# Forming the leaky-ReLU activation in place in PSUM for every tile, with both float32r parts read from there

## The chip, the cores and the metric

One Trainium2 chip; the program runs on one of its cores. The metric is the device time of one execution in microseconds (us). The engines are TensorE (PE, with its weight loads PEld), VectorE (DVE), ScalarE (ACT), GpSimd (POOL) and SyncE (SP), which issues all the DMAs. Each of them works through its own queue in order; semaphores tie the queues together.

## What is computed

A two-step packed attention for 8 batches of 8 heads (576 tokens, head dimension 64, 32 packing queries), and behind it a feed-forward layer with a leaky ReLU whose slope alpha differs by feature:

```python
def _attn_ref(q, k, v, p):
    p_packed = sm_attn(p, k, v)                 # softmax attention of the 32 packing queries
    return sm_attn(q, p_packed, p_packed)       # then of the 576 queries over the 32 results

def _moe_ref(x, w_in, w_out, alpha):            # x: 4608 x 512, w_in: 512 x 2048, w_out: 2048 x 512
    h = x @ w_in
    g = np.maximum(h, 0.0) + alpha * np.minimum(h, 0.0)
    return g @ w_out
```

## The kernel before

The feed-forward layer is cut into 256 tiles (k, f): k is one of 16 half batches of 288 tokens (HS), f one of 16 blocks of 128 features. `first` computes a tile's h into a PSUM tile `ps_h`, of which there are two (`ps_h` pool, bufs=2), forms the activation from it, and splits it into two float32r parts, gh (high) and gl (low, the remainder). `second` multiplies both parts by the split output weights and adds into the four PSUM tiles acc0 to acc3: for each of four column blocks two matmuls with gh (L516, L517) and one with gl (L518), 12 a tile. `first` takes 6 matmuls a tile (L480 to L482), each of 288 columns; in the 32 tiles of batch 0 (k < 2) it takes two float32 matmuls (L468) in their place.

The activation of a tile is formed in one of two ways, by the tile's place i in the order:

- i < 32: DVE computes neg = min(h, 0) * alpha (L487) and g = max(h, 0) + neg (L491), both from ps_h, g into SBUF.
- otherwise: ACT computes neg = Relu(-h) (L495) and g = Relu(h) (L496), both from ps_h into SBUF, and DVE g = neg * (-alpha) + g (L497), all in SBUF.

Then ACT casts g to gh (L502), and gl = g - gh (L504) is POOL's for i < 48 and DVE's from there on. ps_h is free for the tile after next when its last reader is done: the second DVE step in the first way, the second Relu in the other.

Beside the tiles run generators that the main loop steps by the table `plan`: `w_out_steps` and `packed_w(..., True)`, which turn the 64-bit weights into two float32r parts (`convert`: ACT L117, L119, L133, DVE L120, L123, L127, L131, L134) during the first 32 tiles; `attention` for the batches ahead, with its splits on POOL (xl L173, vs L275, a_l L392), its softmax steps on DVE, ACT and POOL (L371, L378), and its score sums on DVE (s and s_t, L211); and `packed_w`, which multiplies the attention's results into the input weights (pw), which `split_pw` splits into pwh (DVE L456) and pwl (L458, POOL for k < 4, else DVE).

The loop emits first(i) and then second(i - 2) (AHEAD = 2). The order in which an engine gets its instructions is not the order of the code: the tile framework's scheduler places each instruction by its own timeline of when operands and buffers come free.

Of the kernel before, what the change touches and what calls it, by code (L numbers as in the profile page):

```python
# [8 lines left out]
F32 = mybir.dt.float32  # L9
# [3 lines left out]
AF = mybir.ActivationFunctionType  # L13
ALU = mybir.AluOpType
# [8 lines left out]
def fv(ap):  # L23

    return ap.bitcast(F32)
# [3 lines left out]
def pack_attention_ffn_kernel(  # L29
# [20 lines left out]
    nc = tc.nc  # L50

    B, NP, P, S = qT.shape
    N = pT.shape[-1]
    KT = (S + P - 1) // P
    HS = S // 2
# [18 lines left out]
    gp = ctx.enter_context(tc.tile_pool(name="gp", bufs=2))  # L74
    op = ctx.enter_context(tc.tile_pool(name="op", bufs=2))
# [13 lines left out]
    al = const.tile([P, NF], F32, name="al")  # L89
    nal = const.tile([P, NF], F32, name="nal")  # L90
# [360 lines left out]
    def split_pw(k, h):  # L451

        src = pw[k // 2, h // 2][:, :, (h % 2) * 256 : (h % 2) * 256 + 256]
        th = pwj.tile([P, 2, 256], F32R, name="pwh", tag="pwh")
        tl = pwj.tile([P, 2, 256], F32R, name="pwl", tag="pwl")
        nc.vector.tensor_copy(out=th, in_=src)  # L456
        eng = nc.gpsimd if k < 4 else nc.vector
        eng.tensor_tensor(out=tl, in0=src, in1=fv(th), op=ALU.subtract)  # L458
        pj[k, h] = (th, tl)

    def first(k, f):
        tok = slice((k % 2) * HS, (k % 2) * HS + HS)
        ps = ps_h.tile([P, 512], F32, name="ps_h", tag="h")
        if k < 2 * XF:
            th, a_f = pw[k // 2, f // 4], result[k // 2]
            fs = slice((f % 4) * P, (f % 4) * P + P)
            for i in range(2):
                nc.tensor.matmul(  # L468
                    ps[:, :HS], th[:, i, fs], a_f[:, i, tok], start=(i == 0), stop=(i == 1)
                )  # L470
        else:
            a_h, a_l = result[k // 2]
            key = (0 if k < 2 else k, f // 2)
            if key not in pj:
                split_pw(*key)
            th, tl = pj[key]
            fs = slice((f % 2) * P, (f % 2) * P + P)
            for i in range(2):
                hi, lo = (i == 0), (i == 1)
                nc.tensor.matmul(ps[:, :HS], th[:, i, fs], a_h[:, i, tok], start=hi, stop=False)  # L480
                nc.tensor.matmul(ps[:, :HS], th[:, i, fs], a_l[:, i, tok], start=False, stop=False)  # L481
                nc.tensor.matmul(ps[:, :HS], tl[:, i, fs], a_h[:, i, tok], start=False, stop=lo)  # L482
        i = order.index((k, f))
        neg = gp.tile([P, HS], F32, name="neg", tag="neg")
        g = gp.tile([P, HS], F32, name="g", tag="g")
        if 0 <= i < 32:
            nc.vector.tensor_scalar(  # L487
                out=neg, in0=ps[:, :HS], scalar1=0.0, scalar2=al[:, f : f + 1],
                op0=ALU.min, op1=ALU.mult,
            )  # L490
            nc.vector.scalar_tensor_tensor(  # L491
                out=g, in0=ps[:, :HS], scalar=0.0, in1=neg, op0=ALU.max, op1=ALU.add
            )
        else:
            nc.scalar.activation(out=neg, in_=ps[:, :HS], func=AF.Relu, scale=-1.0)  # L495
            nc.scalar.activation(out=g, in_=ps[:, :HS], func=AF.Relu)  # L496
            nc.vector.scalar_tensor_tensor(  # L497
                out=g, in0=neg, scalar=nal[:, f : f + 1], in1=g, op0=ALU.mult, op1=ALU.add
            )
        gh = gp.tile([P, HS], F32R, name="gh", tag="gh", bufs=3)  # L500
        gl = gp.tile([P, HS], F32R, name="gl", tag="gl", bufs=3)
        nc.scalar.copy(out=gh, in_=g)  # L502
        eng = nc.gpsimd if 0 <= i < 48 else nc.vector
        eng.tensor_tensor(out=gl, in0=g, in1=fv(gh), op=ALU.subtract)  # L504
        gs[k, f] = (gh, gl)

    def second(k, f):
# [32 lines left out]
    order = [(h, 4 * j + f) for j in range(NJ) for h in range(2) for f in range(4)]  # L540
# [27 lines left out]
            yield  # L568

    nc.sync.dma_start(out=al, in_=alpha)  # L570
    nc.vector.tensor_scalar(out=nal, in0=al, scalar1=-1.0, scalar2=None, op0=ALU.mult)

    w0 = packed_w([0], units(*range(NJ)), True)
    drain(zipped(attention(0, 0, True), after(3, attention(0, 1, True))))
# [22 lines left out]
    order = [(h, 4 * j + f) for j in range(NJ) for h in range(2) for f in range(4)]  # L597
    order += [(k, f) for k in range(2, 2 * B) for f in range(NF)]
    AHEAD = 2
    for i in range(len(order) + AHEAD):  # L600
        now = [gen for t, gen, n in plan for _ in range(max(1, -n)) if t <= i and (n < 0 or (i - t) % n == 0)]
        for gen in now[0::2]:
            next(gen, None)
        if i < len(order):
            first(*order[i])
        for gen in now[1::2]:
            next(gen, None)
        if i >= AHEAD:
            second(*order[i - AHEAD])
# [35 lines left out]
```

## Time and profile before

| | us |
|---|---|
| median of 3 runs | 842.3 (841.11 to 844.02) |
| the profiled execution | 844.03 |
| its span, first to last instruction | 842.0 |
| PE busy (matmuls) | 788.6 (94%) |
| DVE busy | 661.8 (79%) |
| ACT busy | 545.1 (65%) |
| POOL busy | 260.1 (31%) |

The shares are means over stages with different limits: in the 40 equal slices of the span DVE is at nine tenths or more from 21 us to 168 us and again in single slices between 270 and 590 us, POOL in the one slice from 232 to 253 us, and PE in nearly all slices from 210 us to the end (not around 390 and 580 us). The chain of work that ended last runs 69% of the span over PE and 16% over DVE. The granted TensorE clock is at nine tenths or more in all slices but the second and the third; over the span it is 0.978. The times in the rows further down are all of this one execution.

### The profile page before, as it was taken

To read this page: it belongs to the slowest core of one execution; us is meant where nothing else is said; L and a number is where in the kernel's file an instruction comes from. 1 tells how busy PE (TensorE), PEld (TensorE's weight loads), DVE (VectorE), ACT (ScalarE), POOL (GpSimd) and SP (SyncE) were. 2 spreads that over 40 slices of the span, in tenths; PEclk is the share of its full clock that TensorE was granted. 3 is DMA by queue.
4 is the path that set the end of the run, shared out by engine and by line. 5 is a ranking of instruction groups with operands and counts; after the bars stand their busy time and mean duration, and the time that the engine had idled before them with its cause. 6 is when DMAs were issued, how large, how long until landed. Compare 5 with 4: busy or idle time off the path is not lost.

```text
span 842.0 us, 15167 instructions
## 1 busy us (share of the span) xinstructions
PE 788.6 (94%) x5384; PEld 733.9 (87%) x5384; DVE 661.8 (79%) x1287; ACT 545.1 (65%) x1333; POOL 260.1 (31%) x251
## 2 busy tenths in 40 slices
PE   5489989898999999998999999997999999999997
PEld 3257767787799999998999999997999999999997
DVE  4999999965788857889989848889889656666663
ACT  5767656556776796667676787665665874545443
POOL 2122234667895511344335302244232100000000
PEclk9879999999999999999999999999999999999999
DMA  9766755556623582312122572211000640000000
GB/s 305 271 213 223 242 184 192 184 157 211 205 68 111 156 244 75 89 46 69 42 61 71 179 238 83 71 57 52 34 16 29 206 148 1 30 1 29 1 30 28
DMA packets 55386, 97.97 MB, mean 116 GB/s; under 512 B 5136, under 2 KB 32784, under 8 KB 55312
## 3 DMA queue, kind: packets, MB, share of 16 engines
q1 hardware_dynamic: 55312, 97.02, 36.0%
q8 instruction: 42, 0.69, 0.4%
q14 instruction: 32, 0.26, 0.1%
HBM read 79.18 MB, written 17.83 MB: 115 GB/s over the span
## 4 chain that ended last, share of the span: by engine, by line
PE 69%; DVE 16%; ACT 6%; DMA 4%; issue 3%; POOL 1%; SPq 1%; ACTq 0%; DVEq 0%; POOLq 0%
PE acc L516 13%; PE acc L518 13%; PE acc L517 13%; PE ps_h L482 6%; PE ps_h L480 6%; PE ps_h L481 6%; DVE g L497 2%; PE ps_h L468 2%; PE ps_m L435 2%; DVE gl L504 1%; PE ps_m L437 1%; PE ps_m L316 1%; PE ps_m L436 1%; DVE mag L127 1%; DVE pwl L458 1%
## 5 line engine op out<-in xcount | busy, mean ns | idle before, releaser
L516 PE MATMUL acc<-gh,wo 128*128 128x288 f32 x1024 | 301.0, 303 | 6.6 <-ACT gh L502 3.9
L517 PE MATMUL acc<-gh,wo 128*128 128x288 f32 x1024 | 296.3, 297 | 0.0
L518 PE MATMUL acc<-gl,wo 128*128 128x288 f32 x1024 | 263.2, 299 | 2.4 <-DVE gl L504 1.7
L516 PEld LDWEIGHTS acc<-gh,wo 128*128 128x128 f32 x1024 | 193.1, 189 | 15.3 <-ACT gh L502 6.2
L517 PEld LDWEIGHTS acc<-gh,wo 128*128 128x128 f32 x1024 | 193.3, 189 | 2.4
L502 ACT CAST gh<-g 128x288 fp32r<-128x288 f32 x256 | 110.1, 433 | 124.0 <-DVE g L497 107.3
L518 PEld LDWEIGHTS acc<-gl,wo 128*128 128x128 f32 x1024 | 179.4, 189 | 7.8 <-DVE gl L504 3.3
L504 DVE TENSOR_TENSOR gl<-g,gh 128x288 fp32r<-128x288 f32 x208 | 123.9, 598 | 60.3 <-ACT gh L502 56.8
L497 DVE SCALAR_TENSOR_TENSOR g<-neg,nal,g 128x288 f32<-128x288 f32 x224 | 133.5, 598 | 38.1 <-ACT g L496 36.9
L480 PE MATMUL ps_h<-a_h,pwh 128*128 128x288 f32 x448 | 132.9, 297 | 0.4 <-DVE pwh L456 0.4
L481 PE MATMUL ps_h<-a_l,pwh 128*128 128x288 f32 x448 | 132.4, 296 | 0.0
L482 PE MATMUL ps_h<-a_h,pwl 128*128 128x288 f32 x448 | 131.7, 295 | 0.0
L495 ACT ACTIVATE neg<-ps_h 128x288 f32<-128x288 f32 x224 | 92.2, 412 | 50.5 <-PE ps_h L482 46.8
L173 POOL TENSOR_TENSOR xl<-xraw,xh 128x576 fp32r<-128x576 f32 x48 | 72.5, 1512 | 153.9 <-ACT xh L172 151.9
L496 ACT ACTIVATE g<-ps_h 128x288 f32<-128x288 f32 x224 | 91.1, 408 | 14.5 <-DVE gl L504 12.9
L480 PEld LDWEIGHTS ps_h<-a_h,pwh 128*128 128x128 f32 x448 | 84.7, 189 | 1.5 <-DVE pwh L456 0.7
L481 PEld LDWEIGHTS ps_h<-a_l,pwh 128*128 128x128 f32 x448 | 84.7, 189 | 0.3
L482 PEld LDWEIGHTS ps_h<-a_h,pwl 128*128 128x128 f32 x448 | 84.3, 189 | 0.4
L458 DVE TENSOR_TENSOR pwl<-pw,pwh 128x512 fp32r<-128x512 f32 x96 | 76.1, 793 | 5.4
L456 DVE CAST pwh<-pw 128x512 fp32r<-128x512 f32 x112 | 61.5, 552 | 12.2 <-PE ps_h L481 9.4
L443 ACT COPY pw<-ps_m 64x512 f32<-64x512 f32 x112 | 65.0, 581 | 7.0 <-PE ps_m L437 5.6
L504 POOL TENSOR_TENSOR gl<-g,gh 128x288 fp32r<-128x288 f32 x48 | 45.0, 947 | 68.1 <-ACT gh L502 65.0
(116 smaller groups left out, 1154.0 us busy)
## 6 DMA issues: line engine op xcount, KB each, us to landing
w<-w_split SPq DMA_DIRECT2D x64, 512.0 KB, 4.1
xraw<-in_kT SPq DMA_DIRECT2D x32, 288.0 KB, 2.9
xraw<-in_qT SPq DMA_DIRECT2D x32, 288.0 KB, 2.9
outT<-ot SPq DMA_DIRECT2D x64, 144.0 KB, 1.8
vraw<-in_v SPq DMA_DIRECT2D x32, 256.0 KB, 2.9
wraw<-in_w_out SPq DMA_DIRECT2D x16, 512.0 KB, 4.1
wraw<-in_w_in SPq DMA_DIRECT2D x16, 512.0 KB, 5.0
w_split<-w SPq DMA_DIRECT2D x16, 512.0 KB, 3.8
```

The source lines that it names most:

```text
L458: eng.tensor_tensor(out=tl, in0=src, in1=fv(th), op=ALU.subtract)
L480: nc.tensor.matmul(ps[:, :HS], th[:, i, fs], a_h[:, i, tok], start=hi, stop=False)
L481: nc.tensor.matmul(ps[:, :HS], th[:, i, fs], a_l[:, i, tok], start=False, stop=False)
L482: nc.tensor.matmul(ps[:, :HS], tl[:, i, fs], a_h[:, i, tok], start=False, stop=lo)
L495: nc.scalar.activation(out=neg, in_=ps[:, :HS], func=AF.Relu, scale=-1.0)
L496: nc.scalar.activation(out=g, in_=ps[:, :HS], func=AF.Relu)
L497: nc.vector.scalar_tensor_tensor(out=g, in0=neg, scalar=nal[:, f : f + 1], in1=g, op0=ALU.mult, op1=ALU.add)
L502: nc.scalar.copy(out=gh, in_=g)
L504: eng.tensor_tensor(out=gl, in0=g, in1=fv(gh), op=ALU.subtract)
L516: nc.tensor.matmul(acc[o][:, :HS], wo_t[f][:, 0, os_], gh, start=begin, stop=False)
L517: nc.tensor.matmul(acc[o][:, :HS], wo_t[f][:, 1, os_], gh, start=False, stop=False)
L518: nc.tensor.matmul(acc[o][:, :HS], wo_t[f][:, 0, os_], gl, start=False, stop=end)
```

## The change

In all 256 tiles the activation is now formed in one way: ACT computes neg = Relu(-h) from ps_h into SBUF (L486), DVE computes neg * (1 - alpha) + h with ps_h as its second operand and writes the result back to ps_h (L487), ACT casts gh from ps_h (L492), and DVE computes gl from ps_h and gh (L493). The second Relu, the SBUF tile g, the way with two DVE steps and POOL's gl are gone. The constant nal becomes 1 - alpha in the one instruction that made -alpha. ps_h is free for the tile after next when gl is done.

```diff
-        i = order.index((k, f))
         neg = gp.tile([P, HS], F32, name="neg", tag="neg")
-        g = gp.tile([P, HS], F32, name="g", tag="g")
-        if 0 <= i < 32:
-            nc.vector.tensor_scalar(
-                out=neg, in0=ps[:, :HS], scalar1=0.0, scalar2=al[:, f : f + 1],
-                op0=ALU.min, op1=ALU.mult,
-            )
-            nc.vector.scalar_tensor_tensor(
-                out=g, in0=ps[:, :HS], scalar=0.0, in1=neg, op0=ALU.max, op1=ALU.add
-            )
-        else:
-            nc.scalar.activation(out=neg, in_=ps[:, :HS], func=AF.Relu, scale=-1.0)
-            nc.scalar.activation(out=g, in_=ps[:, :HS], func=AF.Relu)
-            nc.vector.scalar_tensor_tensor(
-                out=g, in0=neg, scalar=nal[:, f : f + 1], in1=g, op0=ALU.mult, op1=ALU.add
-            )
+        g = ps[:, :HS]
+        nc.scalar.activation(out=neg, in_=g, func=AF.Relu, scale=-1.0)
+        nc.vector.scalar_tensor_tensor(
+            out=g, in0=neg, scalar=nal[:, f : f + 1], in1=g, op0=ALU.mult, op1=ALU.add
+        )
         gh = gp.tile([P, HS], F32R, name="gh", tag="gh", bufs=3)
         gl = gp.tile([P, HS], F32R, name="gl", tag="gl", bufs=3)
         nc.scalar.copy(out=gh, in_=g)
-        eng = nc.gpsimd if 0 <= i < 48 else nc.vector
-        eng.tensor_tensor(out=gl, in0=g, in1=fv(gh), op=ALU.subtract)
+        nc.vector.tensor_tensor(out=gl, in0=g, in1=fv(gh), op=ALU.subtract)
...
-    nc.vector.tensor_scalar(out=nal, in0=al, scalar1=-1.0, scalar2=None, op0=ALU.mult)
+    nc.vector.tensor_scalar(out=nal, in0=al, scalar1=-1.0, scalar2=1.0, op0=ALU.mult, op1=ALU.add)
```

The scheduler makes another order of this. In the rows that follow, square brackets name the engines (or DMA queues) whose semaphores an instruction waits for. PE's queue before, in the last half batch (k = 15): ps_h_11060 is the h of f = 14, wo12 the output weights of f = 12.

```order
L518 MATMUL acc3_10719<-gl_10985,wo11_1214 128x288
L480 MATMUL ps_h_11060<-a_h_7829,pwh_11061 128x288 [waits Activation_49]
L481 MATMUL ps_h_11060<-a_l_7830,pwh_11061 128x288
L482 MATMUL ps_h_11060<-a_h_7829,pwl_11062 128x288
L480 MATMUL ps_h_11060<-a_h_7829,pwh_11061 128x288
L481 MATMUL ps_h_11060<-a_l_7830,pwh_11061 128x288
L482 MATMUL ps_h_11060<-a_h_7829,pwl_11062 128x288
L516 MATMUL acc0_10716<-gh_11016,wo12_1312 128x288 [waits Activation_49]
L517 MATMUL acc0_10716<-gh_11016,wo12_1312 128x288
L516 MATMUL acc1_10717<-gh_11016,wo12_1312 128x288
L518 MATMUL acc0_10716<-gl_11017,wo12_1312 128x288 [waits DVE_49]
```

The same place now: ps_h_10614 is the h of f = 15, wo13 the output weights of f = 13.

```order
L505 MATMUL acc3_10265<-gh_10568,wo13_1397 128x288
L506 MATMUL acc3_10265<-gh_10568,wo13_1397 128x288
L480 MATMUL ps_h_10614<-a_h_7551,pwh_10585 128x288 [waits DVE_49]
L481 MATMUL ps_h_10614<-a_l_7552,pwh_10585 128x288
L482 MATMUL ps_h_10614<-a_h_7551,pwl_10586 128x288
L480 MATMUL ps_h_10614<-a_h_7551,pwh_10585 128x288
L481 MATMUL ps_h_10614<-a_l_7552,pwh_10585 128x288
L482 MATMUL ps_h_10614<-a_h_7551,pwl_10586 128x288
L507 MATMUL acc0_10262<-gl_10569,wo13_1397 128x288
L507 MATMUL acc1_10263<-gl_10569,wo13_1397 128x288
L507 MATMUL acc2_10264<-gl_10569,wo13_1397 128x288
L507 MATMUL acc3_10265<-gl_10569,wo13_1397 128x288
```

Before, first waits for ACT (the second Relu of the tile that had the bank) and stands ahead of the whole second step of the tile two back. Now it waits for DVE (gl of that tile) and stands between that tile's gh matmuls and its gl matmuls; in most of the 256 tiles the order reads gh x8, first x6, gl x4.

DVE's queue among the first 32 tiles before, where the weights are converted beside them (mag is the convert's working tile, w and wo its low parts, pt the attention's result):

```order
L491 SCALAR_TENSOR_TENSOR g_1025<-ps_h_1021,neg_1024 128x288 [waits DVE_49,Pool_49]
L127 SCALAR_TENSOR_TENSOR mag_841<-wraw13_839,mag_841 128x512 [waits DMAHW0_49,DVE_49]
L123 TENSOR_SCALAR mag_873<-mag_873 128x512 [waits DVE_49]
L120 TENSOR_SCALAR mag_946<-mag_946 128x512 [waits Activation_49]
L131 ISA mag_841<-mag_841,low_843 128x1024 [waits DVE_49]
L127 SCALAR_TENSOR_TENSOR mag_873<-wraw14_871,mag_873 128x512 [waits DMAHW2_49,DVE_49]
L123 TENSOR_SCALAR mag_946<-mag_946 128x512 [waits DVE_49]
L487 TENSOR_SCALAR neg_1082<-ps_h_1079,al_108 128x288 [waits PE_49]
L131 ISA mag_873<-mag_873,low_875 128x1024 [waits DVE_49]
L134 TENSOR_TENSOR w_849<-mag_841,w_849 128x512 [waits DMAHW7_49,Activation_49]
L127 SCALAR_TENSOR_TENSOR mag_946<-wraw11_944,mag_946 128x512 [waits DMAHW3_49,DVE_49]
L491 SCALAR_TENSOR_TENSOR g_1083<-ps_h_1079,neg_1082 128x288 [waits DVE_49,Pool_49]
```

and now:

```order
L493 TENSOR_TENSOR gl_859<-ps_h_852,gh_858 128x288 [waits PE_49,Activation_49]
L487 SCALAR_TENSOR_TENSOR ps_h_896<-neg_899,nal_109,ps_h_896 128x288 [waits Activation_49]
L131 ISA mag_833<-mag_833,low_835 128x1024 [waits DVE_49]
L120 TENSOR_SCALAR mag_864<-mag_864 128x512 [waits Activation_49]
L123 TENSOR_SCALAR mag_864<-mag_864 128x512 [waits DVE_49]
L120 TENSOR_SCALAR mag_936<-mag_936 128x512 [waits Activation_49]
L127 SCALAR_TENSOR_TENSOR mag_864<-wraw14_862,mag_864 128x512 [waits DMAHW1_49,DVE_49]
L123 TENSOR_SCALAR mag_936<-mag_936 128x512 [waits DVE_49]
L355 TENSOR_TENSOR pt_112<-p2f_114,pt_112 128x64 [waits Activation_49] x2
L493 TENSOR_TENSOR gl_903<-ps_h_896,gh_902 128x288 [waits PE_49,Activation_49]
L131 ISA mag_864<-mag_864,low_866 128x1024 [waits DVE_49]
L127 SCALAR_TENSOR_TENSOR mag_936<-wraw11_934,mag_936 128x512 [waits DMAHW6_49,DVE_49]
```

Of the two DVE steps of a tile the first waited for PE and the other for DVE and POOL; now the first waits for ACT's neg, the second, gl, for ACT's gh, and convert steps stand between them as before.

POOL's queue from the first tile on, before (t, a_l and vs are the attention's tiles, vraw a raw v):

```order
L504 TENSOR_TENSOR gl<-g,gh 128x288 x9
L181 MEMSET vraw 64x128
L504 TENSOR_TENSOR gl<-g,gh 128x288 x2
L181 MEMSET vraw 64x128
L504 TENSOR_TENSOR gl<-g,gh 128x288 x5
L371 TENSOR_TENSOR t_1074<-t_1074,m_1076 128x576
L504 TENSOR_TENSOR gl<-g,gh 128x288 x2
L378 TENSOR_TENSOR t_1074<-t_1074,z_1128 128x576
```

and now:

```order
L181 MEMSET vraw 64x128 x2
L371 TENSOR_TENSOR t_1062<-t_1062,m_1064 128x576
L378 TENSOR_TENSOR t_1062<-t_1062,z_1115 128x576
L181 MEMSET vraw 64x128
L392 TENSOR_TENSOR a_l<-s_948,a_h 128x576
L181 MEMSET vraw 64x128
L275 TENSOR_TENSOR vs<-vraw,vs 128x5x128
```

The 48 gl are gone from POOL; what is left are the attention's steps and the zeroing of vraw's ends.

## Rows read from the trace of the kernel before

**Rows 1.** Windows: busy us (instructions) of PE PEld DVE ACT POOL, clock, DMA, GB/s.

```profile
44.00:173.00 129.00, 117.20 (x610) 90.44 (x610) 125.19 (x244) 82.10 (x176) 49.44 (x48) 0.93 0.64 208
173.00:250.00 77.00, 69.98 (x472) 62.27 (x471) 54.95 (x103) 52.92 (x132) 62.88 (x59) 1.00 0.53 166
250.00:372.00 122.00, 121.01 (x880) 118.57 (x880) 96.34 (x184) 90.26 (x223) 42.95 (x40) 1.00 0.40 121
372.00:402.00 30.00, 27.28 (x201) 26.35 (x200) 28.68 (x50) 20.05 (x52) 15.42 (x13) 1.00 0.23 70
402.00:566.00 164.00, 162.63 (x1188) 158.93 (x1188) 134.96 (x265) 114.56 (x293) 49.21 (x46) 1.00 0.33 101
566.00:592.00 26.00, 21.35 (x137) 20.35 (x136) 25.03 (x40) 14.91 (x38) 13.27 (x9) 0.90 0.20 58
592.00:665.00 73.00, 73.00 (x537) 72.08 (x536) 62.26 (x126) 48.12 (x125) 18.77 (x17) 0.99 0.16 53
665.00:842.00 177.00, 171.19 (x1267) 169.54 (x1266) 101.94 (x213) 94.13 (x238) 0.00 (x0) 0.99 0.12 41
```

**Rows 2.** Lines by shape, whole span: busy us, mean ns, idle before.

```profile
L497 DVE SCALAR_TENSOR_TENSOR g<-neg,nal,g 128x288 f32<-128x288 f32 x224 | 133.5, 598 | 38.1 <-ACT g L496 36.9
...
L504 DVE TENSOR_TENSOR gl<-g,gh 128x288 fp32r<-128x288 f32 x208 | 123.9, 598 | 60.3 <-ACT gh L502 56.8 <-PE ps_h L482 0.9 <-PE acc L518 0.9
...
L487 DVE TENSOR_SCALAR neg<-ps_h,al 128x288 f32<-128x288 f32 x32 | 16.0, 502 | 0.9 <-PE ps_h L468 0.8
...
L491 DVE SCALAR_TENSOR_TENSOR g<-ps_h,neg 128x288 f32<-128x288 f32 x32 | 14.2, 445 | 0.3
```

**Rows 3.** Lines by shape, DVE, 665 to 842 us.

```profile
L497 DVE SCALAR_TENSOR_TENSOR g<-neg,nal,g 128x288 f32<-128x288 f32 x69 | 35.5, 514 | 22.0 <-ACT g L496 21.8
L504 DVE TENSOR_TENSOR gl<-g,gh 128x288 fp32r<-128x288 f32 x70 | 32.9, 472 | 32.3 <-ACT gh L502 30.8 <-PE ps_h L482 0.9
```

**Rows 4.** Lines by shape, DVE, 566 to 592 us.

```profile
L504 DVE TENSOR_TENSOR gl<-g,gh 128x288 fp32r<-128x288 f32 x7 | 5.0, 718 | 0.7 <-ACT gh L502 0.5
L497 DVE SCALAR_TENSOR_TENSOR g<-neg,nal,g 128x288 f32<-128x288 f32 x7 | 4.6, 662 | 0.0
...
L211 DVE TENSOR_TENSOR s_t<-ps_m,lo 64x288 f32<-64x288 f32 x4 | 1.7, 446 | 0.1
```

**Rows 5.** Lines by shape, DVE, 372 to 402 us.

```profile
L497 DVE SCALAR_TENSOR_TENSOR g<-neg,nal,g 128x288 f32<-128x288 f32 x10 | 7.0, 708 | 0.0
L504 DVE TENSOR_TENSOR gl<-g,gh 128x288 fp32r<-128x288 f32 x8 | 6.0, 754 | 0.4 <-ACT gh L502 0.4
```

**Rows 6.** Lines by shape, 173 to 250 us, DVE, then POOL.

```profile
L497 DVE SCALAR_TENSOR_TENSOR g<-neg,nal,g 128x288 f32<-128x288 f32 x17 | 16.1, 963 | 1.5 <-ACT g L496 1.4
...
L504 POOL TENSOR_TENSOR gl<-g,gh 128x288 fp32r<-128x288 f32 x18 | 15.4, 875 | 3.8 <-ACT gh L502 3.8
```

**Rows 7.** Lines by shape, DVE, 0 to 44 us, then 44 to 173.

```profile
L127 DVE SCALAR_TENSOR_TENSOR mag<-wraw,mag 128x512 uint32<-128x512 uint32 x6 | 4.0, 674 | 0.0
L123 DVE TENSOR_SCALAR mag<-mag 128x512 uint32<-128x512 uint32 x8 | 3.9, 500 | 0.1
...
L127 DVE SCALAR_TENSOR_TENSOR mag<-wraw,mag 128x512 uint32<-128x512 uint32 x26 | 20.1, 775 | 0.0
...
L123 DVE TENSOR_SCALAR mag<-mag 128x512 uint32<-128x512 uint32 x24 | 15.3, 636 | 0.0
```

**Rows 8.** Lines by shape, POOL, 44 to 173 us.

```profile
L504 POOL TENSOR_TENSOR gl<-g,gh 128x288 fp32r<-128x288 f32 x30 | 29.6, 990 | 64.3 <-ACT gh L502 61.2 <-PE acc L517 2.9
```

**Rows 9.** Timeline, DVE, ACT: start, duration (us), instruction, idle before.

```profile
573.51 1.65 DVE L497 SCALAR_TENSOR_TENSOR g<-neg,nal,g 128x288 f32<-128x288 f32 x1
...
575.19 0.43 ACT L502 CAST gh<-g 128x288 fp32r<-128x288 f32 x1 [2.66 <-DVE g L497]
```

**Rows 10.** Timeline, ACT, a tile in the last stage.

```profile
700.41 0.41 ACT L495 ACTIVATE neg<-ps_h 128x288 f32<-128x288 f32 x1 [0.18 <-PE ps_h L482]
...
701.71 0.43 ACT L502 CAST gh<-g 128x288 fp32r<-128x288 f32 x1 [0.59 <-DVE g L497]
```

## The prediction, made before the changed kernel ran

> **What bounds the kernel now.** I read the table of windows first, since no share over the whole span says what one stage is worth [rows 1]. From 665 us on PE is the bound: 1267 matmuls in 171.2 us of 177, 135 ns each, and the rest is the last output's way out. 250 to 372, 402 to 566 and 592 to 665 us look the same: PE is idle for 1.0, 1.4 and 0.0 us. Four stretches are different. From 44 to 173 us DVE is busy for 125.2 of 129 us and PE idle for 11.8: DVE sets the pace of the first 32 tiles, as it converts the weights beside them. From 173 to 250 us POOL is busy for 62.9 of 77 us and PE idle for 7.0. From 372 to 402 and from 566 to 592 us DVE is busy for 28.7 of 30 and 25.0 of 26 us, and PE idle for 2.7 and 4.7. That is 28.6 us of idle PE in all between 44 and 665 us; the matmuls' recorded spans overlap, so short gaps between them are hidden and the true loss is somewhat larger. No change to the activation can win much more than that, and after 665 us it can win nothing.
>
> Then I read what the activation's steps cost, by line and shape [rows 2], and the same lines stage by stage. Both DVE steps with two SBUF operands, g (L497) and gl (L504), average 598 ns; where POOL is silent they take 514 and 472 [rows 3], from 566 to 592 us 662 and 718 [rows 4], from 372 to 402 us 708 and 754 [rows 5], from 173 to 250 us g takes 963 [rows 6]. So POOL stretches them. The steps that read one operand from PSUM are not stretched: s_t at 64x288, in the same 26 us in which gl takes 718, takes 446 [rows 4], and over the run g from ps_h (L491) takes 445 and neg from ps_h, with a pointer scalar, 502 [rows 2].
>
> **The change part by part.**
>
> New g. One SBUF tensor (neg), one PSUM tensor, a pointer scalar, and its output goes to PSUM. No row shows a DVE write to PSUM. Bounds: 445 ns (L491, PSUM in, no pointer) and 963 (the dearest g, rows 6); nothing suggests less than 445, since the length is the same 288. I take 502, the nearest row: PSUM in, a pointer scalar, the same length.
>
> New gl: one PSUM tensor, one SBUF tensor, out to SBUF. L491 is that form: 445 ns, so I take 445; the upper bound is the old quiet 472.
>
> The Trainium skill speaks against this. Its page "VectorE: DVE Perf Modes", section "The TRN2 errata — SBUF-src ops pay a fixed extra latency per instruction", prices a PSUM-source DVE instruction 62 cycles of 0.96 GHz above an SBUF-source one, an estimated 65 ns. By it the 17 g and 15 gl of the two crowded stretches would save 2 us less, and the sum would come out at about 828. The rows show 445 with one operand in PSUM against 472 with both in SBUF, so I do not take it.
>
> First 32 tiles, 44 to 173 us. DVE loses neg (502) and g (445) and gets g (502) and gl (445): nothing, net. ACT gets one neg a tile, 32 x 0.41 = 13 us on 82 of 129 busy: covered, if its queue is not late. What POOL does there stretches the convert's DVE steps. Two of their five lines, here and before 44 us [rows 7]: L127 775 against 674, x26, L123 636 against 500, x24: 2.6 + 3.3 = 5.9 us of stretch. POOL loses 30 gl of 990 ns, 29.6 of its 49.4 us [rows 8], 60% of its work, so about 3.5 us of these come back, and perhaps as much again on the three lines not counted. Against it stands that DVE, in order, now waits for ACT's gh between g and gl: in the quiet stretch 30.8 us over 70 tiles, 0.44 each [rows 3]; here converts stand between the two in the queue and cover it. I take 6 of the 11.8 us.
>
> Tiles 32 to 47, 173 to 250 us. POOL loses 18 gl, 15.4 of its 62.9 us [rows 1, 6]. DVE gets 18 x 0.445 = 8.0 and loses 17 x (963 - 502) = 7.8 on g: even. ACT loses a 0.41 us step a tile. POOL is no longer the bound, DVE at 55 of 77 is not either. I take 6 of PE's 7.0 us and of the short gaps that the records hide.
>
> Tiles from 48 on. In the two crowded stretches DVE saves 10 x (708 - 502) + 8 x (754 - 445) = 4.5 us [rows 5] and 7 x (662 - 502) + 7 x (718 - 445) = 3.0 us [rows 4], 7.5 us where PE is idle for 7.4. A place in point: at 573.5 us one g takes 1.65 us and ACT stands 2.66 us waiting for it [rows 9]. I take 6. Elsewhere in this stage DVE and ACT (one step fewer, 0.41 us a tile) get slack that PE does not need: 0. After 665 us: 0.
>
> nal gets a second operation in its one instruction: 0. The pool g gives up its SBUF: 0.
>
> Sum: 6 + 6 + 6 = 18 us off the profiled execution's 844.0 gives **826.0 us**. That execution lies 1.7 us above the median of the runs, 842.3; the sum is not finer than that.
>
> **Rivals.**
>
> *The bank is held too long (slower).* Before, the second Relu frees the ps_h bank; now gl does, three hand-overs later. There are two banks. PE's order, shown above with the change, turns round: first waited for ACT and stood ahead of the second step of the tile two back; now it waits for DVE's gl and stands behind that tile's gh matmuls. From the end of first to its own gh matmuls there were 36 matmuls, now 22: 4.9 us and 3.0 us at 135 ns. To the reuse of the bank there are 30, 4.0 us, and that now has to hold neg, g, gh and gl: 0.41 + 0.50 + 0.43 + 0.45 = 1.8 us in the quiet stretch, with the bounds taken above for g and gl [rows 2, 3, 10], so the tail is safe. In the crowded stages a tile takes about 2.9 us, so the bank gives 2 x 2.9 less first's 6 x 0.135, 5.0 us. It decides from the point where the chain exceeds 5.0 us; each us beyond costs 0.5 us a tile. A chain that twice meets a wait like the 2.66 us above takes 7.1 us and costs 1.05 us. If one in seven of the some 140 tiles between 250 and 665 us does, that is 21 us; with 12 won earlier and nothing in the crowded stretches the time is 844 - 12 + 21 = 853. For it: two banks, and queues that are in order on both sides. Against it: g and gl themselves no longer stretch, ACT has a third less to do for a tile. The same case covers a dear write to PSUM: at 963 ns the 32 first tiles alone lose 15 us. The Trainium skill's page "PSUM — Partial Sum Buffer", summary of rules, says to evacuate promptly, which is this rival in one word.
>
> *The first stage gives nothing (small gain).* DVE's order there is bound to ACT twice a tile in place of once. With 0.3 us of uncovered wait on each of 32 tiles the 6 us turn to a loss of 3, and some of the rest goes too: 844 + 3 - 10 = 837.
>
> *All idle PE comes back.* 844.0 - 28.6 = 815, and the hidden gaps carry it to about 808.
>
> *It does nothing that can be measured.* The gains above and the bank's waits cancel: 842.
>
> **How the numbers follow.** The forecast (818 to 834) gets 0.43, the small gain (834 to 839.8) 0.20, all idle PE (below 818) 0.12, no difference 0.08, the bank 0.17. A measurement of this kernel can tell about 0.3% from no change, 839.8 to 844.8 around the median. Faster is 0.43 + 0.20 + 0.12 = 0.75, the same 0.08, slower 0.17. The range has to leave out no more than 0.2: from 810 (half of the third case out, 0.06) to 848 (two thirds of the bank's case out, 0.11).
>
> **What would show it.** g and gl near 500 and 445 ns in every stage, with and without POOL beside them; the convert's L123 and L127 nearer to 500 and 674; POOL below 50 of 77 us from 173 to 250 us; the stage up to the 32nd tile about 6 us shorter; no change in the pace of the last 64 tiles. Wrong if g into PSUM is above 600 ns, or if waits of first (L480) on DVE's gl show up as idle PE between 250 and 665 us.

## The result, and the profile after

The changed kernel takes 832.7 us (median of 4 runs, 831.57 to 834.60) beside 843.2 us for the kernel before on the same chip: a ratio of 0.9877, 95% interval 0.9844 to 0.9910, so 10.5 us less. The profiled execution is 834.6 us with a span of 832.8 (before 844.0 and 842.0).

The windows of the kernel after, with the edges of [rows 1] and their columns (us, then busy us of PE, PEld, DVE, ACT, POOL with instructions, clock, DMA share, GB/s):

```profile
44.00:173.00 129.00, 120.60 (x633) 92.97 (x632) 117.36 (x251) 94.28 (x215) 25.83 (x22) 0.95 0.66 217
173.00:250.00 77.00, 73.36 (x513) 67.66 (x512) 55.40 (x128) 49.39 (x120) 44.95 (x43) 1.00 0.50 161
250.00:372.00 122.00, 120.01 (x869) 116.88 (x868) 88.67 (x187) 79.65 (x184) 46.58 (x43) 1.00 0.39 121
...
402.00:566.00 164.00, 158.95 (x1146) 154.69 (x1145) 125.37 (x275) 103.66 (x245) 58.01 (x53) 0.99 0.33 104
566.00:592.00 26.00, 26.00 (x202) 26.00 (x201) 19.69 (x45) 13.96 (x37) 7.06 (x8) 1.00 0.10 33
...
665.00:833.00 168.00, 161.75 (x1211) 160.48 (x1210) 100.81 (x207) 57.20 (x144) 0.00 (x0) 1.00 0.05 19
```

Beside [rows 1]: PE does 633 and 513 instructions in the first two stretches, where it did 610 and 472. From 250 to 372 and from 402 to 566 us it does fewer than before, 869 for 880 and 1146 for 1188, although DVE and ACT have less to do there. The gap at 566 to 592 us is gone, and others have opened.

The costliest groups of the page after (line, engine, operation, tiles and shape, count | busy us, mean ns | idle time before them and what ended it):

```profile
L505 PE MATMUL acc<-gh,wo 128*128 128x288 f32 x1024 | 289.6, 302 | 11.0 <-ACT gh L492 7.9
...
L505 PEld LDWEIGHTS acc<-gh,wo 128*128 128x128 f32 x1024 | 193.0, 189 | 24.1 <-ACT gh L492 15.8
...
L493 DVE TENSOR_TENSOR gl<-ps_h,gh 128x288 fp32r<-128x288 f32 x256 | 115.4, 452 | 72.1 <-ACT gh L492 70.4
L487 DVE SCALAR_TENSOR_TENSOR ps_h<-neg,nal,ps_h 128x288 f32<-128x288 f32 x256 | 132.0, 516 | 44.9 <-ACT neg L486 43.3
```

g took 598 ns and takes 516, gl 598 and 452 [rows 2]. PE waits longer for ACT's gh at the first matmuls of `second`: 15.8 us before the weight loads of L505, where the same place of the kernel before (L516) had 6.2:

```profile
L516 PEld LDWEIGHTS acc<-gh,wo 128*128 128x128 f32 x1024 | 193.1, 189 | 15.3 <-ACT gh L502 6.2
```

Where in the run the time went is read from the ends of the 256 casts to gh (one a tile, in order; tile 0 is the first). The table holds the end of that cast for tiles 31, 48 and 255, and the two differences; all kernels of the study but the pair with a third bank stand in it, since it is read again below. Each row is one execution, the profiled one; 28 executions of the kernel before, taken beside e7, e9 and e11, spread from 839.9 to 848.1 us, so a difference of two or three us in one row says little.

| kernel | way in tiles 0-31 / 32-47 / 48-255 | tile 31 | tile 48 | tile 255 | 31 to 48 | 48 to 255 |
|---|---|---|---|---|---|---|
| before | old, POOL gl / old, POOL gl / old | 178.9 | 250.4 | 833.4 | 71.4 | 583.0 |
| after | in place in all | 178.2 | 242.0 | 824.9 | 63.8 | 583.0 |
| e1 | g to SBUF in all | 179.0 | 247.8 | 822.5 | 68.8 | 574.7 |
| e2 | old, gl always on DVE | 182.0 | 251.5 | 843.8 | 69.6 | 592.3 |
| e3 | in place / in place / old | 175.7 | 240.8 | 824.2 | 65.0 | 583.5 |
| e4 | old / old / in place | 178.3 | 247.3 | 830.6 | 69.0 | 583.3 |
| e6 | g to SBUF / in place / in place | 177.6 | 246.4 | 828.9 | 68.8 | 582.5 |
| e7 | two DVE steps, DVE gl / in place / in place | 184.5 | 253.2 | 837.6 | 68.7 | 584.4 |
| e8 | in place / in place / g to SBUF | 176.9 | 240.7 | 812.5 | 63.8 | 571.8 |
| e9 | old / in place / in place | 180.5 | 251.2 | 832.8 | 70.7 | 581.6 |
| e11 | as e8, but gl reads ps_h | 175.7 | 239.5 | 829.6 | 63.8 | 590.1 |

Before against after: tile 31 ends 0.7 us earlier, tile 48 8.4 us, tile 255 8.5 us. Nearly all of the gain shows between tiles 31 and 48, and 208 of the 256 tiles win nothing.

### The profile page after: what moved, and what is told of

It is laid out like the page before. It is cut to its first block, busy times and chain, and to the rows that moved or that the text cites. A ratio compares the mean times of both kernels' runs of the same rounds, so it can differ in the third digit from the quotient of the medians.

```text
span 832.8 us, 14967 instructions
## 1 busy us (share of the span) xinstructions
PE 786.3 (94%) x5384; PEld 731.3 (88%) x5384; DVE 610.6 (73%) x1303; ACT 486.6 (58%) x1141; POOL 208.7 (25%) x203
## 4 chain that ended last, share of the span: by engine, by line
PE 71%; DVE 14%; DMA 6%; ACT 5%; issue 2%; SPq 1%; POOL 0%; ACTq 0%; DVEq 0%
PE acc L505 14%; PE acc L506 13%; PE acc L507 13%; PE ps_h L480 6%; PE ps_h L482 6%; PE ps_h L481 6%; PE ps_h L468 2%; PE ps_m L435 2%; PE ps_m L437 2%; PE ps_m L436 2%; DVE ps_h L487 2%; DMA wraw<-in_w_in 1%; PE ps_m L316 1%; DVE pwl L458 1%; DVE mag L127 1%
## 5 line engine op out<-in xcount | busy, mean ns | idle before, releaser
L505 PE MATMUL acc<-gh,wo 128*128 128x288 f32 x1024 | 289.6, 302 | 11.0 <-ACT gh L492 7.9
L506 PE MATMUL acc<-gh,wo 128*128 128x288 f32 x1024 | 283.4, 295 | 0.0
L505 PEld LDWEIGHTS acc<-gh,wo 128*128 128x128 f32 x1024 | 193.0, 189 | 24.1 <-ACT gh L492 15.8
L507 PE MATMUL acc<-gl,wo 128*128 128x288 f32 x1024 | 205.9, 301 | 0.0
L492 ACT CAST gh<-ps_h 128x288 fp32r<-128x288 f32 x256 | 102.5, 401 | 123.8 <-DVE ps_h L487 113.2
L486 ACT ACTIVATE neg<-ps_h 128x288 f32<-128x288 f32 x256 | 105.6, 413 | 109.0 <-PE ps_h L482 103.0
L493 DVE TENSOR_TENSOR gl<-ps_h,gh 128x288 fp32r<-128x288 f32 x256 | 115.4, 452 | 72.1 <-ACT gh L492 70.4
L487 DVE SCALAR_TENSOR_TENSOR ps_h<-neg,nal,ps_h 128x288 f32<-128x288 f32 x256 | 132.0, 516 | 44.9 <-ACT neg L486 43.3
L507 PEld LDWEIGHTS acc<-gl,wo 128*128 128x128 f32 x1024 | 159.3, 188 | 3.5
L480 PE MATMUL ps_h<-a_h,pwh 128*128 128x288 f32 x448 | 133.5, 298 | 0.3 <-DVE gl L493 0.2
L480 PEld LDWEIGHTS ps_h<-a_h,pwh 128*128 128x128 f32 x448 | 84.1, 188 | 2.0 <-DVE gl L493 1.0
L456 DVE CAST pwh<-pw 128x512 fp32r<-128x512 f32 x112 | 54.9, 493 | 29.9 <-PE ps_h L481 27.7
L275 POOL TENSOR_TENSOR vs<-vraw,vs 128x640 fp32r<-128x640 f32 x24 | 38.6, 1610 | 42.3 <-ACT vs L274 41.7
L435 PE MATMUL ps_m<-w,pt 128*128 128x512 f32 (+1 forms) x80 | 33.8, 422 | 12.9 <-ACT w L133 10.6
```

The source lines that it names most:

```text
L486: nc.scalar.activation(out=neg, in_=g, func=AF.Relu, scale=-1.0)
L487: nc.vector.scalar_tensor_tensor(out=g, in0=neg, scalar=nal[:, f : f + 1], in1=g, op0=ALU.mult, op1=ALU.add)
L493: nc.vector.tensor_tensor(out=gl, in0=g, in1=fv(gh), op=ALU.subtract)
L505: nc.tensor.matmul(acc[o][:, :HS], wo_t[f][:, 0, os_], gh, start=begin, stop=False)
L506: nc.tensor.matmul(acc[o][:, :HS], wo_t[f][:, 1, os_], gh, start=False, stop=False)
L507: nc.tensor.matmul(acc[o][:, :HS], wo_t[f][:, 0, os_], gl, start=False, stop=end)
```

## The experiments

Two theories went in, A and B in the expectations. A, *DVE and POOL work:* the gain is POOL's gl gone and DVE's steps out of POOL's way. B, *held bank:* on top of that, holding ps_h until gl gives part of it back. Ratios are to the kernel before on the same chip.

**e1: g to SBUF in all tiles**, so that the bank is free after g.

```diff
-        g = ps[:, :HS]
-        nc.scalar.activation(out=neg, in_=g, func=AF.Relu, scale=-1.0)
+        g = gp.tile([P, HS], F32, name="g", tag="g")
+        nc.scalar.activation(out=neg, in_=ps[:, :HS], func=AF.Relu, scale=-1.0)
         nc.vector.scalar_tensor_tensor(
-            out=g, in0=neg, scalar=nal[:, f : f + 1], in1=g, ...
+            out=g, in0=neg, scalar=nal[:, f : f + 1], in1=ps[:, :HS], ...
```

> The changed kernel, but DVE writes g to an SBUF tile in place of ps_h; gh and gl are made from there. The bank is free after DVE's g, two hand-overs earlier than in the changed kernel, and gl has two SBUF operands again. Theory A (the win comes from DVE's and POOL's work alone, the bank costs nothing): gl goes back to about 600 ns where POOL works, g stays near 510, the time is 834 to 838 us. Theory B (holding the bank gives part of the win back, since first waits for gl and PE reaches a tile's gh matmuls after 22 matmuls in place of 36): PE's idle time before the gh matmuls falls from 35 us (weight loads and matmuls) to the 22 us of the kernel before, the first 32 tiles end 3 us or more sooner than in the changed kernel, and the time is 824 to 830 us.

Measured: 833.0 us, 0.9864 (0.9843 to 0.9885), the same as the change. Under the same total lie two opposite moves. From 240 to 660 us, e1's groups of weight loads, then of DVE:

```profile
L505 PEld LDWEIGHTS acc<-gh,wo 128*128 128x128 f32 x576 | 108.2, 188 | 1.9 <-DVE ot L524 0.9
...
L480 PEld LDWEIGHTS ps_h<-a_h,pwh 128*128 128x128 f32 x286 | 53.7, 188 | 5.7 <-DVE g L487 5.2
```

```profile
L493 DVE TENSOR_TENSOR gl<-g,gh 128x288 fp32r<-128x288 f32 x145 | 90.6, 626 | 29.3 <-ACT gh L492 27.8
L487 DVE SCALAR_TENSOR_TENSOR g<-neg,nal,ps_h 128x288 f32<-128x288 f32 x144 | 72.5, 506 | 18.0 <-ACT neg L486 17.2
```

and the weight loads of the same stretch in the changed kernel, then the gh ones of the kernel before:

```profile
L505 PEld LDWEIGHTS acc<-gh,wo 128*128 128x128 f32 x560 | 105.9, 189 | 10.5 <-ACT gh L492 8.1 <-ACT ot L522 0.5 <-DVE ot L524 0.4
...
L480 PEld LDWEIGHTS ps_h<-a_h,pwh 128*128 128x128 f32 x280 | 52.6, 188 | 1.2 <-DVE gl L493 0.7 <-DVE den L263 0.3
```

```profile
L516 PEld LDWEIGHTS acc<-gh,wo 128*128 128x128 f32 x564 | 106.5, 189 | 4.8 <-ACT gh L502 2.0 <-DVE ot L535 0.9 <-ACT ot L533 0.9
```

In e1 gl is stretched again, 626 ns. From the change to e1, PE's idle time ahead of the gh matmuls falls from 10.5 us (8.1 of it for gh) to 1.9, and that ahead of `first` (L480) rises from 1.2 to 5.7, nearly all of it for the g that frees the bank. By the table e1 wins 8.3 us behind tile 48 and loses 5.8 ahead of it. So a smaller amount of DVE work does not by itself make PE faster late in the run.

**e2: the kernel before, with gl on DVE in all tiles.**

```diff
-        eng = nc.gpsimd if 0 <= i < 48 else nc.vector
+        eng = nc.vector
```

> The kernel before with one edit: gl is DVE's in all tiles, in place of POOL's in the first 48. Theory A: POOL is relieved, but DVE, 97% busy in the first 32 tiles, gets 32 x 0.46 = 15 us more there with nothing taken away; tiles 32 to 47 win some 4 us: 850 to 856 us, slower. If POOL's stretch of DVE's convert steps is worth more than that (theory C), the time is at or below 843 us.

Measured: 854.8 us, 1.0135 (1.0106 to 1.0164). Taking gl off POOL alone costs 11 us. In the change ACT takes over one of the three DVE steps that this leaves to each of the first 32 tiles; e7, below, keeps all three on DVE there and loses the whole gain. About 1 us of the 11 lies ahead of tile 48 and 9 behind it, where the code is that of the kernel before. The scheduler's order is another there, and e2 comes to tile 48's cast with less of the other work done: 343 matmuls into ps_m, the attention's PSUM tile, for 350, and 324 DVE steps that belong to no tile for 332. Which of the two costs the 9 us is not told apart. So the time behind tile 48 can move by some us without any edit there, and a single row of the table is no proof of a few.

**e3 and e4: the change in tiles 0 to 47 alone, and in tiles 48 to 255 alone.**

```diff
-        g = ps[:, :HS]
+        i = order.index((k, f))
...
+        inplace = i < 48        # e4: i >= 48
+        if inplace:
+            g = ps[:, :HS]
...
+        else:                   # the kernel before's two ways, and its gl
```

> The change in the tiles i < 48 alone; the others keep the two Relus, g in SBUF and the earlier release of the bank. Theory A and the stage table: nearly all of the win lies in these tiles, 832 to 836 us. Theory B adds that the later tiles lose nothing to the held bank here: 830 to 833, at or below the changed kernel.

> The change in the tiles i >= 48 alone; the first 48 are as in the kernel before. The prediction's term for the crowded stretches: 6 us off 843, 837. The stage table of the changed kernel, in which short gaps lose 18 us between 250 and 650 us against 21 before: 1 to 4 us off, 839 to 842. Theory B in its strong form (the held bank costs as much as DVE wins): 843 or above.

Measured: e3 835.5 us, 0.9894 (0.9874 to 0.9914); e4 840.4 us, 0.9955 (0.9939 to 0.9971). The first 48 tiles carry most of it. e4's 3.8 us are not won in the tiles that it changes: behind tile 48 it takes 583.3 us, the kernel before 583.0.

**e8: in place in the first 48 tiles, g to SBUF from there on.**

```diff
-        g = ps[:, :HS]
+        late = order.index((k, f)) >= 48
+        h = ps[:, :HS]
+        g = gp.tile([P, HS], F32, name="g", tag="g") if late else h
```

> In place for the first 48 tiles; from tile 48 on the same two DVE steps, but g goes to SBUF, so that ps_h is free after g and not after gl. Theory 'held bank': in the first 48 tiles the short in-place steps are worth having (e3: 0.9894), and from 250 us on it is the held bank that makes PE wait for gh; the gap that the changed kernel has there (20.3 us) falls to what e1 had (12 us) while its early stretch (34.7 us against e1's 37.5) stays: 825 to 829 us, ratio 0.978 to 0.983. Rival 'only the amount of DVE and POOL work counts': e1 and the changed kernel took the same time because the release of the bank does nothing in either part, so any mix of them takes it too: 831 to 835 us, ratio 0.985 to 0.989.

Measured: 823.8 us (822.2 to 826.8), 0.9771 (0.9746 to 0.9795): 19 us under the kernel before and about 9 under the changed kernel, the best of the study, and a little below what *held bank* expected. e1's late gain and the change's early gain add up, as *held bank* says and *DVE and POOL work* does not.

**e11: e8, with one operand changed.**

```diff
-        nc.vector.tensor_tensor(out=gl, in0=g, in1=fv(gh), op=ALU.subtract)
+        nc.vector.tensor_tensor(out=gl, in0=h, in1=fv(gh), op=ALU.subtract)
```

> e8 with one edit: the late tiles' gl reads ps_h in place of g, so gl is h - gh there and the output is not the reference's. It holds the bank until gl as the changed kernel does, while g still goes to SBUF, gh is still cast from SBUF and gl is again the unstretched 450 ns step: less DVE work than e8, and a longer hold. Theory 'held bank': all of e8's gain over the changed kernel is lost, 830 to 835 us, and the weight loads of the gh matmuls wait for gh for 8 us or more between 240 and 660 us. Rival 'the write to PSUM and the reads of g from there are what the late tiles lose by': it keeps e8's gain, 820 to 827 us.

Measured: 839.1 us, 0.9951 (0.9931 to 0.9970), more than was expected and 15 us above e8, for a DVE step that has become cheaper. Windows and weight loads of e8 from 240 to 660 us:

```profile
240.00:660.00 420.00, 417.12 (x3042) 408.64 (x3041) 330.53 (x681) 261.23 (x613) 138.25 (x123) 1.00 0.32 100
```

```profile
L507 PEld LDWEIGHTS acc<-gh,wo 128*128 128x128 f32 x574 | 107.9, 188 | 1.5 <-ACT ot L524 0.3
```

and of e11:

```profile
240.00:660.00 420.00, 409.00 (x2925) 397.38 (x2925) 309.83 (x658) 260.12 (x602) 131.84 (x121) 0.99 0.33 103
```

```profile
L507 PEld LDWEIGHTS acc<-gh,wo 128*128 128x128 f32 x549 | 104.9, 191 | 11.7 <-ACT gh L494 10.0 <-ACT ot L524 0.5
```

DVE is 20.7 us less busy in e11 and PE gets 117 fewer instructions done; PE's idle time ahead of the gh matmuls goes from 1.5 us to 11.7, 10.0 of it for gh. Some of the loss is the granted TensorE clock: it is at the lower of its two levels (1.2 GHz) for 10 of these 420 us in e11, each time next to a wait of PE of 1.7 to 2.2 us, and never in e8, which is up to about 5 us of the 15. Neither the write to PSUM nor ACT's read of g from there is the cause, as g is in SBUF in both. What is left is how long the bank is held, and the order that the scheduler makes of it. The order is visible: in e8, e1 and before, PE has most often 36 matmuls between a tile's `first` and its own gh matmuls (mean over the tiles from 48 on: 42 to 45); in after and in e11 most often 22 (mean 27 to 28), counted in the trace's order of the matmuls. That the wait is shown for gh and not for the bank misleads: `first` stands where its bank is sure to be free, and that is so late that gh is then due too soon.

**h2m1 and h3m1: a third bank.** The two PSUM tiles of the attention's products become one (control), and the tile won becomes a third ps_h.

```diff
-    ps_h = ... bufs=2 ...
-    ps_m = ... bufs=2 ...
+    ps_h = ... bufs=3 ...   # the control leaves this at 2
+    ps_m = ... bufs=1 ...
```

> The changed kernel with one PSUM tile for the attention's products in place of two; ps_h stays at two. It is the control of the next run. Both theories: slower than the changed kernel by 0 to 15 us, since the attention's matmuls now wait for the one tile's readers; 833 to 848 us.

> As the control, but the tile that the attention gave up is a third ps_h. Theory 'held bank': first no longer waits for gl of the tile two back; against the control 5 to 12 us less, of it 3 or more between 44 and 178 us, and L480 and L468 do not wait for DVE's gl. Rival 'the chain neg, g, gh, gl and DVE's queue set the pace, not the bank': within 2 us of the control.

Measured: 976.9 us, 1.158 (1.154 to 1.162), and 1023.1 us, 1.213 (1.210 to 1.217); both expectations fell. Over the run PE's weight loads waited, in the control and then with three banks:

```profile
L505 PEld LDWEIGHTS acc<-gh,wo 128*128 128x128 f32 x1024 | 194.3, 190 | 32.5 <-ACT gh L492 26.4 <-DVE part L518 1.4 <-DVE ot L524 0.9
```

```profile
L505 PEld LDWEIGHTS acc<-gh,wo 128*128 128x128 f32 x1024 | 192.5, 188 | 16.8 <-ACT gh L492 12.5 <-DVE ot L518 1.2 <-DVE ot L524 0.7
```

The third bank halves the idle time ahead of the gh matmuls, with g still in place, and turns the order back: most often 38 and 36 matmuls between a tile's `first` and its gh matmuls from tile 48 on (mean 37), where the control has most often 24 and 22 (mean 25). So it is the bank that sets this order. But with one tile for the attention's products the attention itself holds up PE: the weight loads of one of its products (L207, ps_m<-xh,p) wait 39.0 us in the control and 39.9 with three banks, 0.7 in the change, and PE's mean granted clock falls to 0.90 and 0.88 over the span. Why the third bank makes this 46 us slower still was not looked into. As a price of the bank the pair says nothing; a third bank beside two ps_m was not tried.

**e6, e9 and e7: the first 32 tiles in other ways**, in place from tile 32 on. e6: g to SBUF. e9: the kernel before's way with gl on POOL. e7: the kernel before's two DVE steps with gl on DVE.

```diff
-        g = ps[:, :HS]
+        early = order.index((k, f)) < 32
+        h = ps[:, :HS]
+        g = gp.tile([P, HS], F32, name="g", tag="g") if early else h    # e6
...
+        eng = nc.gpsimd if 0 <= i < 32 else nc.vector                   # e9; e7: nc.vector
```

> The mirror of e8: in the first 32 tiles g goes to SBUF and the bank is free after g; from tile 32 on all in place. Theory 'held bank': if the bank alone holds up the first 32 tiles, releasing it earlier there gives 3 to 5 us: 828 to 830 us. Rival 'in the first stage DVE is the bound, and gl from SBUF is the dearer step there': 833 to 837 us, as the early loss of e1 (37.5 us of gaps from 50 to 250 us against 34.7) says. The first 32 tiles end (end of first of tile 31) before 172 us by the former, after 174 us by the latter.

> The kernel before in the first 32 tiles (two DVE steps, gl on POOL), in place from tile 32 on. It prices the first stage and tiles 32 to 47 apart. The prediction's terms (6 us for each): 6 us above the changed kernel, 839 us, and about 2 us under e4. Rival, from the times of the tiles in the two traces (tile 31 no earlier in the changed kernel, tile 32 to 48 about 5 us earlier): as the changed kernel, 831 to 835 us, so that tiles 32 to 47 carry all that e3 won.

> In the first 32 tiles DVE does all three steps (neg and g from ps_h as before, and gl), in place from tile 32 on: against the changed kernel 0.5 us more of DVE a tile, 16 us in all, and a bank that is free after g. If DVE sets the pace of the first 32 tiles as the prediction says: 8 to 14 us above the changed kernel, 841 to 847 us. If the bank does: it is free earlier, 828 to 834 us.

Measured: e6 839.3 us, 0.9951 (0.9931 to 0.9971); e9 843.2 us, 0.9984 (0.9964 to 1.0004); e7 845.6 us, 1.0017 (0.9996 to 1.0038). By the ratios each is slower than the change, by about 6, 9 and 12 us: the way of the first 32 tiles decides nearly all of the change's gain. e6 lies above both its expectations, nearer to the rival's, and e9 above both of its own. It has the change in 224 tiles, tiles 32 to 47 among them, and no gain that can be told from none. The windows from 115 to 178 us, of the change, of e9 and then of e7:

```profile
115.00:178.00 63.00, 60.05 (x346) 49.17 (x344) 56.26 (x120) 43.40 (x100) 24.69 (x20) 1.00 0.55 185
```

```profile
115.00:178.00 63.00, 54.86 (x290) 44.80 (x289) 56.31 (x110) 34.72 (x74) 31.99 (x31) 0.92 0.49 167
```

```profile
115.00:178.00 63.00, 52.80 (x273) 43.15 (x274) 62.32 (x127) 36.16 (x76) 18.96 (x15) 0.89 0.54 177
```

In e7 DVE is busy for 62.3 of 63 us, PE gets least done, and tile 31 ends 6.3 us later than in the change: with all three steps on DVE, DVE sets the pace of this stage, though e7 frees the bank early and POOL has no gl. Part of what e9 and e7 lose may be the granted clock, 0.92 and 0.89 of these 63 us where the change has 1.00; PE is idle for 8.1 and 10.2 us of them, in the change for 3.0.

## Why the prediction was right, and where its steps failed

The time, 832.7 us, is inside the range (810 to 848), and faster was the likeliest sign. The point forecast, 826.0, was 6.7 us too low. That it came so near is in part luck: of the three terms of 6 us one came, for another reason than the one given, one came as DVE time that ended no tile sooner, and one was taken back by the held bank.

**New g and gl: right.** 516 ns for 502, 452 for 445, in every stage: with 0 to 44 us left out, no stretch of the table of windows has g outside 510 to 519 or gl outside 446 to 457. Of the bounds the lower pair was the one to take. The Trainium skill ("VectorE: DVE Perf Modes", "The TRN2 errata — SBUF-src ops pay a fixed extra latency per instruction") makes a PSUM source dearer by 62 cycles; no run here shows that: in the quiet end g from ps_h takes 519 ns after, the one from SBUF 514 before [rows 3], and gl from ps_h 457 against 458. (The 472 of [rows 3] holds one gl that began ahead of 665 us, beside POOL, and took 1,455 ns; the other 69 average 458.) That POOL stretches steps with two SBUF operands and leaves those with one operand in PSUM alone held throughout: gl is 626 ns in e1 and 451 in the change over the same 420 us. It is also what the Trainium skill says of two SBUF inputs and of at most one ("SBUF — State Buffer", "Who interferes with whom"). It does not follow that one SBUF operand is safe: L123, which reads a single one, takes 411 ns on average where POOL is silent and 902 in the 11 of 24 that overlap a POOL step (44 to 178 us, before); after, the four that overlap one take 418.

**First 32 tiles, 6 us: the saving right, what it buys wrong.** DVE is busy for 117.4 us of the stretch for 125.2 [rows 1], more than the 6 us put down. The convert's lines, DVE, 44 to 173 us after:

```profile
L127 DVE SCALAR_TENSOR_TENSOR mag<-wraw,mag 128x512 uint32<-128x512 uint32 x26 | 19.0, 738 | 0.0
...
L123 DVE TENSOR_SCALAR mag<-mag 128x512 uint32<-128x512 uint32 x25 | 10.3, 416 | 0.1
```

They were 775 and 636 ns [rows 7], so most of it comes from L123. But tile 31 ends only 0.7 us earlier; the stage was forecast to be 6 us shorter. The step that failed: that DVE time won in a stage makes the stage's tiles end sooner. What holds the tiles up is not settled. In places it is the bank, as in this piece of the timeline after (start, duration, engine, line; idle before in brackets):

```profile
66.77 0.52 DVE L487 SCALAR_TENSOR_TENSOR ps_h<-neg,nal,ps_h 128x288 f32<-128x288 f32 x1
...
67.47 1.30 ACT L511 COPY part<-acc 128x288 f32<-128x288 f32 x4
...
68.63 0.46 ACT L492 CAST gh<-ps_h 128x288 fp32r<-128x288 f32 x1
...
69.83 0.45 DVE L493 TENSOR_TENSOR gl<-ps_h,gh 128x288 fp32r<-128x288 f32 x1
...
70.33 1.00 PE L468 MATMUL ps_h<-a_f,pw 128*128 128x288 f32 x3
```

g is ready at 67.3 us; ACT copies part first and casts gh until 69.1, gl ends at 70.28, and the next `first` starts 0.05 us later. But over the stage, 44 to 178 us, the weight loads of `first` wait little for gl (us in total, times, longest):

```profile
PEld ps_h L468 <- DVE gl L493: 1.7, 4, 0.9
```

and e6, whose bank is free after g, ends tile 31 only 0.6 us sooner than the change. So the bank is not shown to set the pace of the stage. What DVE won went into the work beside the tiles. At the end of tile 31's cast PE has done 237 matmuls into ps_m, which belong to no tile, at the same time as 224 before, and DVE 263 other steps as against 254. This work is then not in the way of tiles 32 to 47.

**Tiles 32 to 47, 6 us: the sum nearly right, the cause wrong.** The forecast put it down to POOL's relief, and POOL did fall to 45.0 us of 77 as forecast. e9 relieves POOL there just as much (37.0 us of the 62 from 178 to 240 us, after 36.8), and takes 70.7 us from tile 31 to 48 where before took 71.4; after, e8 and e11, alike in the first 48 tiles, take 63.8. What makes these tiles fast is what was done ahead of them: e6, e7 and e9 have the change's code in these tiles and take 68.7 to 70.7. It goes with the count above. The four kernels with 237 matmuls into ps_m by tile 31's cast (after, e3, e8, e11) take 63.8 to 65.0 us from there to tile 48, the seven with 224 to 229 take 68.7 to 71.4, and at tile 48's cast all but e2 stand at 347 to 350. The windows of this stretch, before and after:

```profile
178.90:250.40 71.50, 65.39 (x443) 58.12 (x442) 52.16 (x97) 51.51 (x128) 61.09 (x57) 1.00 0.53 168
```

```profile
178.20:242.00 63.80, 60.16 (x418) 54.90 (x417) 44.14 (x102) 42.45 (x101) 38.75 (x35) 1.00 0.52 169
```

PE has 25 instructions fewer to do there, is busy for 5.2 us less and idle for 3.6 us in place of 6.1. That the work done ahead is the cause, and not only a sign of it, is argued from this; no run changes that count alone. A POOL that is busy for 62.9 of 77 us was read as a bound, and it was not one. The two terms together were 12 us, and 8.4 came.

**Crowded stretches, 6 us: failed.** DVE did get its time back: from 240 to 660 us its busy time falls from 352.1 us to 311.2. From tile 48 to 255 the kernel takes 583.0 us as before. The rival of the held bank had the mechanism and even the number, 22 matmuls to the own gh where there had been 36, but priced another wait: `first` on gl, with 30 matmuls, 4.0 or 5.0 us, against the whole chain. That wait hardly came (L480 1.2 us above), so the prediction's own sign of this case stayed away while the case was at work. The wait that came is the one of 22 matmuls, 3.0 us, against neg, g and gh: quiet these take 1.3 us (0.41 + 0.52 + 0.40), but more where DVE has other steps queued ahead of g. One such place after; the first row is the last matmul of a tile's `first`:

```profile
533.06 0.30 PE L482 MATMUL ps_h<-a_h,pwl 128*128 128x288 f32 x1
533.88 0.41 ACT L486 ACTIVATE neg<-ps_h 128x288 f32<-128x288 f32 x1
...
535.54 1.89 DVE L458 TENSOR_TENSOR pwl<-pw,pwh 128x512 fp32r<-128x512 f32 x1
...
537.36 0.51 DVE L487 SCALAR_TENSOR_TENSOR ps_h<-neg,nal,ps_h 128x288 f32<-128x288 f32 x1
537.90 0.40 ACT L492 CAST gh<-ps_h 128x288 fp32r<-128x288 f32 x1 [0.87 <-DVE ps_h L487]
...
538.35 0.61 PE L505 MATMUL acc<-gh,wo 128*128 128x288 f32 x1 [2.20 <-ACT gh L492]
```

g stands behind a pwl of 1.89 us, gh is done at 538.30 us, 4.9 us after the end of `first` at 533.36, and PE has waited 2.20 us. So the rival was true in kind, through another wait than the one that it priced at 21 us; in the change it took what the shorter steps had won. Its size stands in the table: with the bank free after g the same tiles take 571.8 us in e8, 11.2 less than in the change, and 18.3 less than in e11. Why e11 takes 7 us more than the change there is not shown. The Trainium skill's rule to evacuate promptly ("PSUM — Partial Sum Buffer", summary of rules) holds there; in the first 32 tiles e6 follows it and is 6 us slower than the change.

**Quiet end, 0:** nearly. From tile 208 to 255 it is 113.4 us after, 112.1 before and 112.4 in e8; L505's weight loads wait 1.3 us for gh there, where L516's had waited 0.2.

**What stays open.** In the first 32 tiles freeing the bank after g is worse (e6, e1), although there too the next `first` waits for gl in the change. e6's first 16 tiles do end earlier (tile 16 at 115.7 us, after 120.4), with less of the other work done (147 matmuls into ps_m at that point, after 166), and its gl and convert steps later meet POOL's attention steps (gl 567 ns from 115 to 178 us, after 445). Whether it is the order or the stretch that costs the 6 us is not told apart.

## What to carry to other kernels

An in-place step in PSUM saved DVE time here, but price what the bank's later release does to the order of the queue: count the matmuls that are left between a tile's first and second step, and hold that against the chain that they must cover. In this kernel the short steps were worth having in the stage in which DVE is busiest, though why e6 loses there is open, and the early release in the stages that TensorE paces; the mixture (e8, 823.8 us) beats both pure forms (832.7 and 833.0). A stage's gain need not show in that stage: look also at how much of the work beside it is done by its end.

## What the runs showed of the hardware

A DVE step of 128x288 that writes its result into PSUM in place takes 516 ns (mean over the run after), into SBUF 507 (e1): the write to PSUM has no price worth a term. ACT's cast of the same tile from PSUM takes 400 ns (240 to 660 us after), from SBUF 433 (e1). And in this kernel one PSUM tile fewer for the attention's products costs 17%: 977 us for 833.
